# Sliding-window attention with a gated MLP on one core: query tiles of two 64-row blocks that lie 128 rows apart, 192 key columns each, in place of 128 consecutive queries with 256 columns

## The chip, the cores and the metric

The kernel runs on one core of a Trainium2 chip. The metric is the device time of one execution in microseconds; the number before is the median of three runs.

## The reference

```python
# q, k, v: batch 8, heads 8, sequence 576, head size 64
rel  = pos[:, None] - pos[None, :]
mask = (rel >= 0) & (rel < 128)
scores = where(mask, q @ k.T / 8 - slope[h] * abs(rel), -1e9)
x = (softmax(scores) @ v).transpose(0, 2, 1, 3).reshape(8, 576, 512)
h = relu(x @ w_in)                  # 512 -> 1024
u, v = h[..., :512], h[..., 512:]
v_n = (v - mean(v)) / sqrt(var(v) + 1e-6)
v_s = einsum('ts,bsd->btd', w_spatial, v_n) + b_spatial[None, :, None]
out = (u * v_s) @ w_out             # 512 -> 512
```

Each query sees itself and the 127 keys before it. A block of 64 queries therefore needs at most 192 keys, a block of 128 consecutive queries at most 256.

## The kernel before, in words

The work of a batch falls into four attention units (one for each pair `p` of heads; `j` is the head in the pair) and a gated part. 576 queries are cut into five tiles of 128, the last of 64. Scores are f32 products with the 64 head dimensions on the partitions, so that both heads and two halves of a query tile fit into the array side by side.

An attention unit of batches 1 to 7 goes through `scores`, `products` and `attention`:

- PE writes the scores of all five tiles in one piece of work (line 641), in blocks of 64 queries and up to 192 keys. Tiles 0 and 1 share one PSUM bank per head, tiles 2 and 3 another (buffers `s`, four of them), and tile 4 takes a buffer `x` (batches from 2 on; in batch 1 it takes `s`). The parts of a 256-column row that no product writes were set to zero once at the start (line 302).
- DVE reads a tile's scores, adds the table of slope and mask for the head (`tabs`), writes the sum to `prob` and keeps the row minimum (line 652). ACT takes the exponential in place, with the row sum (line 658). Both read 128, 256, 256, 256 and 192 columns.
- DVE adds a small constant and takes reciprocals (lines 681, 685). ACT writes the f16 rounding of the normalised probabilities to `pq` (line 693), DVE the remainder (line 698).
- SP transposes all of `pq` of a head by DMA into `pt` (line 704).
- PE multiplies with V in f16 parts (line 737): three products (high and low part of V, high and low part of the probabilities) for each of the seven ranges in `WINDOWS`, which lie in the transposed columns, and for both heads. ACT and DVE split the result into two f16 halves `xt` (lines 746, 750).

Batch 0 and the first pair of batch 1 (the pairs in `RAW` and `first`) take another way, `raw_tile` and `raw_rest`: one tile of one head pair at a time, scores in 128-query products (line 545), `prob` normalised in f32 (lines 577, 578), transposed on PE (line 587), copied to SBUF (line 316) and multiplied with V in f32 (line 605). Beside these tiles run the preparation of the weights, on DVE and ACT.

The gated part (`gated`) holds PE's large products: `v_unit` (line 802), `v_rem` (824), `u_unit` (854), `sp_unit` (875) and `o_unit` (901), with the layer norm (`layer_norm`) between them.

Nothing is issued in source order. Each piece of work is entered in a `Plan` with its engine, an estimated cost, a due time and what it reads and writes. `emit` lists the pieces forwards and backwards 20 times by a model of the engines, with these costs and PE's clock rule in it, and keeps the order that the model ends first. `either` gives a piece two engines, and the model picks one. Costs that a piece is entered with therefore steer the order on all engines and on SP's queue.

Of the kernel before, what the change touches and what calls it, by code (L numbers as in the profile page):

```python
# [9 lines left out]
F32 = mybir.dt.float32  # L10
# [19 lines left out]
MASKED = -2.0 ** 33  # L30
# [143 lines left out]
def attn_gmlp_kernel(ctx, tc, qk, v, w_in, w_spT, b_sp, w_out, outT):  # L174
# [5 lines left out]
    P = 2 * D  # L180
# [26 lines left out]

    RAW = {(0, p) for p in range(4)} | {(1, p) for p in range(1)}
# [8 lines left out]
    plan.kept["s"] = [ps.tile([P, 2, 2 * P], F32, name=f"s{k}") for k in range(4)]  # L217
# [23 lines left out]
    ones = fixed([P, P], BF16, "ones")  # L241
    powers = fixed([P, 2], F32, "powers")
    wpowers = fixed([P, 2], F32, "wpowers")
    tabs = [fixed([P, 2 * P], BF16, f"tab{h}") for h in range(H)]
# [9 lines left out]
    NB = 2 * NQ - 1  # L254
    OFF = [0] + [(2 * t - 1) * P for t in range(1, NQ)]
    prob = [fixed([P, NB * P], F32, f"prob{j}") for j in range(4)]
# [12 lines left out]
    relf = plan.buf(work, "u", 7, [P, 2 * P], F32)  # L269
    maskt = plan.buf(work, "u", 7, [P, 2 * P], F32)  # L270

    def constants():
        def f():
            nc.gpsimd.iota(relf(), [[-1, 2 * P]], base=P, channel_multiplier=1, allow_small_or_imprecise_dtypes=True)
        plan.add("POOL", 400, 0, f, (), [(relf, 0)])

        def f():
            nc.vector.memset(maskt(), 0.0)
        plan.add("DVE", dve(256), 0, f, (), [(maskt, 0)])

        def f():
            nc.gpsimd.affine_select(maskt(), maskt(), [[-1, 2 * P]], ALU.is_ge, MASKED, base=P, channel_multiplier=1)
            nc.gpsimd.affine_select(maskt(), maskt(), [[1, 2 * P]], ALU.is_ge, MASKED, base=-1, channel_multiplier=-1)
        plan.add("POOL", 800, 1, f, [(maskt, 0)], [(maskt, 0)])

        def f():
            nc.vector.memset(ident(), 1.0)
            nc.vector.memset(ones(), 1.0)
            nc.vector.memset(powers()[:, 0:1], 2.0 ** -13)
# [5 lines left out]
        plan.add("DVE", dve(400), 500, f, (), [(ident, 0), (ones, 0), (powers, 0), (wpowers, 0), (nhalf, 0)] + [(rstat, k) for k in range(8)])  # L295
# [5 lines left out]
        for k in range(4):  # L301
            plan.add("DVE", 340, 100, lambda k=k: nc.vector.memset(plan.kept["s"][k][:, 1, :], 0.0))
# [4 lines left out]
        for h in range(H):  # L307
            def f(h=h):
                slope = 2.0 ** (-8.0 * (h + 1) / H)
                nc.vector.scalar_tensor_tensor(tabs[h](), relf(), -8.0 * slope, maskt(), ALU.mult, ALU.add)  # L310
            plan.add("DVE", dve(256), 1000 + h * 4000, f, [(relf, 0), (maskt, 0)], [(tabs[h], 0)])
# [218 lines left out]

    def raw_tile(b, p, t, raw, vb, xt, slot, due, sums=None):

        m, k0, k1 = min(P, S - t * P), max(0, (t - 1) * P), min(S, (t + 1) * P)
        n, c0 = k1 - k0, P if t == 0 else 0
        blocks = [(k, min(P, k1 - k)) for k in range(k0, k1, P)]
        row, NM, SM, TM, RC = (slot + 4 * (t % 2)) % 8, 0, 2, 4, 6
        st = lambda k, j: rstat()[:m, row, k + j:k + j + 1]
        sc = [plan.buf(ps, "s", 4, [P, 2, 2 * P], F32) for _ in range(2)]
        pr = [lambda j=j: prob[2 * (t % 2) + j]()[:m, slot * 2 * P:slot * 2 * P + n] for j in range(2)]
        cols = [parts(prob[2 * (t % 2) + j], slot * 2 * P, slot * 2 * P + n) for j in range(2)]  # L540

        def f():
            for j in range(2):
                rows = slice(j * D, (j + 1) * D)
                nc.tensor.matmul(sc[j]()[:m, 0, :n], raw()[rows, 0, t * P:t * P + m], raw()[rows, 1, k0:k1], start=True, stop=True)
        plan.add("PE", SWITCH // 2 + pe(*[4 * n]), due, f, [(raw, k) for k in range(k0 // P, t + 1)], [(sc[j], 0) for j in range(2)])
        for j in range(2):
            h = 2 * p + j

            def f(j=j, h=h):  # L550
                nc.vector.tensor_tensor_reduce(pr[j](), sc[j]()[:m, 0, :n], tabs[h]()[:m, c0:c0 + n], -0.125, 3e38,
                                               ALU.add, ALU.min, st(NM, j))
            plan.add("DVE", dve(n), due + 300, f, [(sc[j], 0), (tabs[h], 0)], cols[j] + [(rstat, row)])
# [14 lines left out]
    def raw_rest(b, p, t, vb, xt, slot, due, row):  # L568
        m, k0, k1 = min(P, S - t * P), max(0, (t - 1) * P), min(S, (t + 1) * P)
        n = k1 - k0  # L570
        blocks = [(k, min(P, k1 - k)) for k in range(k0, k1, P)]
        RC = 6
        st = lambda k, j: rstat()[:m, row, k + j:k + j + 1]
        pr = [lambda j=j: prob[2 * (t % 2) + j]()[:m, slot * 2 * P:slot * 2 * P + n] for j in range(2)]
        cols = [parts(prob[2 * (t % 2) + j], slot * 2 * P, slot * 2 * P + n) for j in range(2)]
# [4 lines left out]
        tp = plan.buf(ps, *(("m", 2) if b == 0 else ("s", 4)), [P, 2, 2 * P], F32)  # L580
        flat = lambda: tp().rearrange("p a b -> p (a b)")

        def f():
            for i, (k, w) in enumerate(blocks):
                for j in range(2):
                    c = (2 * i + j) * m
                    nc.tensor.transpose(flat()[:w, c:c + m], pr[j]()[:, i * P:i * P + w], ident()[:m, :m])
# [426 lines left out]
```

## Time and profile before

| | |
|---|---|
| median of 3 runs | 585.93 us (585.79 to 586.01) |
| profiled execution | 588.65 us, span 586.9 us |
| PE busy | 554.9 us (95%), 5359 matmuls |
| DVE busy | 497.7 us (85%) |
| ACT busy | 436.9 us (74%) |
| POOL busy | 49.4 us (8%) |
| mean granted TensorE clock | 0.985 |

The span is the time from the first to the last instruction of the profiled execution. A busy share is a mean over stages with different limits, so the stages are looked at one by one below. A matmul's own duration holds its way through the array; neighbours overlap, and the price of one is read from the distance of starts.

### The profile page before, as it was taken

Reading aid. Unit: us, or ns where it says so; the run is one execution under the profiler, and the core shown is the slowest. Engines: PE = TensorE matmul, PEld = TensorE weight load, DVE = VectorE, ACT = ScalarE, POOL = GpSimd, SP = SyncE. Lnnn points to the kernel's source line nnn. Section 1 sums busy time; section 2 is a strip of 40 time slices with the busy share of each in tenths; the row PEclk is TensorE's granted clock in tenths of the full one; section 3 lists DMA queues with packets and bytes.
Section 4 is the critical chain, followed back from the end, with each engine's and each line's share of the span. In section 5 each row is a group of like instructions: output and inputs, shape, how many; then the busy total and the mean of one; then the engine's idle time right before and its main releaser. Section 6 shows DMA issues by size and latency. Waiting matters only on the chain.

```text
span 586.9 us, 14767 instructions
## 1 busy us (share of the span) xinstructions
PE 554.9 (95%) x5359; PEld 413.6 (70%) x5359; DVE 497.7 (85%) x1800; ACT 436.9 (74%) x1379; POOL 49.4 (8%) x108
## 2 busy tenths in 40 slices
PE   3699698999899999999999999999999999999997
PEld 2365346789477876888578957787688957886787
DVE  7989989998899989987998889888999789944650
ACT  5979979996887788877797769779797758743202
POOL 2110021002110001000110001100101011000100
PEclk9999689999899999999999999999999999999999
DMA  8944022489857862694768862886384744451002
GB/s 314 316 172 157 4 91 77 111 194 215 183 104 123 235 160 82 123 231 133 135 124 214 170 150 75 135 222 158 79 155 102 181 92 83 82 120 43 1 11 71
DMA packets 149997, 79.64 MB, mean 136 GB/s; under 512 B 129826, under 2 KB 140066, under 8 KB 149924
## 3 DMA queue, kind: packets, MB, share of 16 engines
q1 hardware_dynamic: 149924, 78.70, 55.4%
q8 instruction: 42, 0.69, 0.5%
q14 instruction: 31, 0.25, 0.2%
HBM read 37.13 MB, written 9.44 MB: 79 GB/s over the span
## 4 chain that ended last, share of the span: by engine, by line
PE 40%; DVE 7%; ACT 3%; DMA 2%; issue 1%; ACTq 0%; DVEq 0%
PE m L875 11%; PE m L901 10%; PE m L854 8%; PE m L802 4%; PE x L737 4%; PE s L641 3%; DMA pt<-pq 2%; DVE st L763 1%; DVE prob L652 1%; ACT junk L516 1%; DVE vt L776 1%; PE m L824 1%; DVE pq L698 1%; DVE vn L813 1%; DMA out_dram<-o 1%
## 5 line engine op out<-in xcount | busy, mean ns | idle before, releaser
L658 ACT ACTIVATE prob<-prob,stat 64x192 f32<-64x192 f32 (+2 forms) x270 | 124.9, 466 | 33.3 <-DVE stat L652 33.1
L875 PE MATMUL m<-wsp,vn 128*128 128x288 f16 x768 | 113.0, 286 | 0.6 <-DVE u L883 0.6
L901 PE MATMUL m<-gs,wout 128*128 128x288 f32 x768 | 110.8, 300 | 0.3 <-DVE o L909 0.3
L693 ACT ACTIVATE pq<-prob,stat 128x128 f16<-128x128 f32 (+1 forms) x270 | 105.8, 467 | 4.3 <-DVE stat L685 4.1
L698 DVE SCALAR_TENSOR_TENSOR pq<-prob,stat,pq 128x128 f16<-128x128 f32 (+1 forms) x270 | 103.5, 435 | 4.0 <-ACT pq L693 3.8
L901 PEld LDWEIGHTS m<-gs,wout 128*128 128x128 f32 x768 | 103.4, 189 | 3.3 <-issue 1.7
L854 PE MATMUL m<-xt,win 128*128 128x288 f16 x768 | 101.3, 286 | 0.9 <-ACT vt L320 0.4
L802 PE MATMUL m<-win,xt 128*128 128x512 f16 x384 | 92.0, 393 | 2.8 <-ACT o L908 2.0
L854 PEld LDWEIGHTS <-win 128*128 128x128 f16 x768 | 73.9, 98 | 24.1 <-issue 4.2
L875 PEld LDWEIGHTS <-vn 128*128 128x128 f16 x768 | 73.1, 98 | 21.7 <-issue 2.9
L652 DVE CUSTOM_DVE_ANT_0 prob<-s,tab 128x256 f32<-128x256 f32 (+2 forms) x222 | 73.1, 380 | 0.1
L802 PEld LDWEIGHTS <-xt 128*128 128x128 f16 x384 | 36.9, 100 | 48.4 <-issue 8.7
L772 POOL TENSOR_TENSOR st<-st,nhalf 128x1 f32<-128x1 f32 (+1 forms) x40 | 25.1, 627 | 315.6 <-DVE st L768 249.2
L658 ACT ACTIVATION_READ_ACCUMULATOR prob<-prob,stat 128x1 f32 (+1 forms) x270 | 51.3, 190 | 0.0
L883 DVE TENSOR_TENSOR u<-m,u 128x288 f32<-128x288 f32 x64 | 28.8, 450 | 23.8 <-PE m L875 23.8
L908 ACT ACTIVATE o<-m,am 128x288 f32<-128x288 f32 x42 | 20.9, 499 | 33.1 <-PE m L901 22.1
L737 PE MATMUL x<-pt,vh 128*64 128x256 f16 (+6 forms) x756 | 42.2, 229 | 1.1 <-DMA pt<-pq 1.0
L641 PE MATMUL s<-qkraw 64*64 64x192 f32 (+2 forms) x876 | 40.2, 310 | 0.0
L320 ACT ACTIVATE u<-m 128x288 f32<-128x288 f32 x57 | 22.9, 401 | 21.1 <-PE m L854 20.9
L737 PEld LDWEIGHTS <-vh 128*64 128x64 f16 x756 | 32.3, 110 | 8.3 <-issue 8.1
L763 DVE BATCH_NORM_STATS2 st<-vt 128x6 f32<-128x512 f32 (+1 forms) x40 | 27.5, 687 | 11.8 <-ACT vt L320 11.5
L737 PE MATMUL x<-pt,vl 128*64 128x256 f16 (+6 forms) x378 | 35.5, 228 | 0.0
(150 smaller groups left out, 808.6 us busy)
## 6 DMA issues: line engine op xcount, KB each, us to landing
qkraw<-in_qk_dram SPq DMA_DIRECT2D x28, 576.0 KB, 4.2
vb<-in_v_dram SPq DMA_DIRECT2D x32, 320.0 KB, 5.8
out_dram<-o SPq DMA_DIRECT2D x64, 144.0 KB, 2.0
vn<-in_w_in_dram SPq DMA_DIRECT2D x8, 512.0 KB, 6.8
pt<-in_w_out_dram SPq DMA_DIRECT2D x4, 512.0 KB, 6.5
gs<-in_w_spT_dram SPq DMA_DIRECT2D x4, 288.0 KB, 8.0
qkraw<-in_qk_dram SPq DMA_DIRECT2D x3, 320.0 KB, 5.4
pt<-pq SPq DMA_TRANSPOSE x54, 4.8
```

Source lines behind the costliest of these rows:

```text
L641: nc.tensor.matmul(sc[k][j]()[out, i, a - k0:z - k0], raw()[rows, 0, q:q + D], raw()[rows, 1, a:z], start=True, stop=True, skip_group_chec ...
L652: nc.vector.tensor_tensor_reduce(pt(), sc()[:m, i, :n], tabs[h]()[:m, c0:c0 + n], -0.125, 3e38, ALU.add, ALU.min, st()[:m, NM, j, t:t + 1])
L658: nc.scalar.activation(pt(), pt(), AF.Exp, bias=st()[:m, NM, j, t:t + 1], scale=-1.0, accum_out=st()[:m, SM, j, t:t + 1])
L693: nc.scalar.activation(pq[j]()[:m, 0, cs], prob[2 * (p % 2) + j]()[:m, cs], AF.Copy, scale=st()[:m, RC, j, t:t + 1])
L698: nc.vector.scalar_tensor_tensor(pq[j]()[:m, 1, cs], prob[2 * (p % 2) + j]()[:m, cs], st()[:m, RC, j, t:t + 1], pq[j]()[:m, 0, cs], ALU.mu ...
L737: nc.tensor.matmul(xp()[j * D:(j + 1) * D, x0:x0 + n], l()[:, kt, j * D:(j + 1) * D], rhs[:, o:o + n], start=j not in seen, stop=False, sk ...
L763: nc.vector.bn_stats(st()[:m, 0:6], vt()[:m])
L802: nc.tensor.matmul(pt(), xt[c]()[:, X0[a] + t * P:X0[a] + (t + 1) * P], win()[:, c, w, DH:DF], start=(n == 0), stop=(n == 3 * NC_ - 1))
L854: nc.tensor.matmul(pt()[:, :HS], win()[:, c, w, d * P:(d + 1) * P], xt[c]()[:, X0[a] + hf * HS:X0[a] + (hf + 1) * HS], start=(n == 0), sto ...
L875: nc.tensor.matmul(pt()[:, :HS], l, r, start=(n == 0), stop=(n == len(ops) - 1))
L883: nc.vector.tensor_tensor(u(), pt()[:, :HS], u(), ALU.mult)
L901: nc.tensor.matmul(pt()[:, :HS], wout()[:, d, w, e * P:(e + 1) * P], gs[d]()[:, a, :], start=(n == 0), stop=(n == 3 * ND - 1))
```

## The change: other query tiles

With nine blocks of 64 queries (0 to 8), the tiles become block 0 alone, and the pairs (1, 3), (2, 4), (5, 7) and (6, 8). The two blocks of a pair lie 128 rows apart, so that both have their keys in ranges of 192 columns that begin at different keys but have the same place relative to the queries; one table serves both. There are still five tiles. Block 1 has only 128 keys; the 64 columns ahead of them are filled by a small bf16 product (`ones` with `masked`), once per head.

```diff
+    TILES = ((0,), (1, 3), (2, 4), (5, 7), (6, 8))
+    W = P + D
+    POFF = (0, D, D + W, D + 2 * W, D + 3 * W)
+    QOFF = (0, 3 * D, 6 * D, 11 * D, 14 * D)
+    QGAPS = ((0, 3 * D), (9 * D, 11 * D), (17 * D, 18 * D))
+    SOFF = (0, D, D + W, 0, W)
...
-            nc.gpsimd.iota(relf(), [[-1, 2 * P]], base=P, channel_multiplier=1, allow_small_or_imprecise_dtypes=True)
...
-            nc.gpsimd.affine_select(maskt(), maskt(), [[-1, 2 * P]], ALU.is_ge, MASKED, base=P, channel_multiplier=1)
-            nc.gpsimd.affine_select(maskt(), maskt(), [[1, 2 * P]], ALU.is_ge, MASKED, base=-1, channel_multiplier=-1)
...
+            for a in (0, D):
+                rel = relf()[a:a + D]
+                nc.gpsimd.iota(rel, [[-1, W]], base=P, channel_multiplier=1, allow_small_or_imprecise_dtypes=True)
+                nc.gpsimd.affine_select(rel, rel, [[-1, W]], ALU.is_ge, FAR, base=P, channel_multiplier=1)
+                nc.gpsimd.affine_select(rel, rel, [[1, W]], ALU.is_ge, FAR, base=-1, channel_multiplier=-1)
...
-        for k in range(4):
-            plan.add("DVE", 340, 100, lambda k=k: nc.vector.memset(plan.kept["s"][k][:, 1, :], 0.0))
...
-                nc.vector.scalar_tensor_tensor(tabs[h](), relf(), -8.0 * slope, maskt(), ALU.mult, ALU.add)
-            plan.add("DVE", dve(256), 1000 + h * 4000, f, [(relf, 0), (maskt, 0)], [(tabs[h], 0)])
+                nc.gpsimd.tensor_scalar(tabs[h](), relf(), -8.0 * slope, None, ALU.mult)
...
+                nc.vector.tensor_scalar(tabs[h](), relf(), -8.0 * slope, None, ALU.mult)
+            plan.either([("DVE", dve(W, True), fv)] + [("POOL", pool(W), f)] * (h > 1), 1000 + h * 1000, [(relf, 0)], [(tabs[h], 0)])
...
+    def keys(i):
+        return max(0, i - 2) * D, (i + 1) * D
+
+    def scored(sc, t, off, raw):
+
+        for x, i in enumerate(TILES[t]):
+            k0, k1 = keys(i)
+            at = off + (W if t else D) - (k1 - k0)
+            out = slice(x * D, (x + 1) * D)
+            for j in range(2):
+                rows = slice(j * D, (j + 1) * D)
+                if at > off:
+                    nc.tensor.matmul(sc[j]()[out, off:at], ones()[rows, :D], masked()[rows], start=True, stop=True, skip_group_check=True)
+                nc.tensor.matmul(sc[j]()[out, at:at + k1 - k0], raw()[rows, 0, i * D:(i + 1) * D], raw()[rows, 1, k0:k1],
+                                 start=True, stop=True, skip_group_check=True)
+
+    def scored_ns(t):
+        return 107 if t == 0 else 360 if t == 1 else 320
...
+        plan.add("PE", SWITCH // 2 + scored_ns(t), due, lambda: scored(sc, t, 0, raw), seen_by(raw, t) + [(ones, 0), (masked, 0)], [(sc[j], t) for j in range(2)])
...
-        if len({w for _, w in blocks}) == 1:
-            e = len(blocks) * 2 * m
-            copy(e, lambda: (pf(P, 0, e), flat()[:, :e]), due + 1500, [(tp, 0)], pcols)
...
+        if t:
+            copy(2 * m, lambda: (pf(slice(0, P), 0, 2 * m), tp()[:, 0:2 * m]), due + 1500, [(tp, 0)], pcols[:len(pcols) // 2])
+        copy(2 * m, lambda: (pf(half, 2 * m, 4 * m), tp()[0:D, 2 * m:4 * m]), due + 1500, [(tp, 0)], halves)
...
-    BANKS = (((0, 1), ("s", 4)), ((2, 3), ("s", 4)), ((4,), ("x", 2)))
-
-    WINDOWS = (((0, 0, 256, 0), (1, 256, 160, 128), (2, 512, 32, 256)),
-               ((1, 416, 96, 0), (2, 544, 224, 0), (3, 768, 192, 96), (4, 1024, 64, 224)))
+    MOVES = ((0, 2, 0, 1, 2), (0, 0, 0, 0, 1), (0, 1, D, 3, 1), (1, 2, D, 3, 2), (1, 4, 0, 2, 1), (2, 4, D, 4, 1),
+             (1, 5, 0, 5, 1), (2, 6, 0, 5, 2), (2, 5, D, 7, 1), (3, 6, D, 7, 2), (3, 8, 0, 6, 1), (4, 8, D, 8, 1))
...
-                d = due - 4500 + (t if len(banks) < 3 or t < NQ - 1 else -1) * 700 + j * 200
...
+                d = due - 4500 + t * 700 + j * 200
...
-        for g, banks in enumerate((BANKS,) if b >= WHOLE else (BANKS[:2], ((BANKS[2][0], ("s", 4)),))):
+        for g, banks in enumerate((((0, 1, 2), (3, 4)),) if b >= WHOLE else (((0, 1, 2),), ((3, 4),))):
...
+            for kt, chunk, c, i, n in MOVES:
+                xp, x0 = xps[i > 4], (i - 5 * (i > 4)) * D
+                for l, a in ((vh, 0), (vh, 1), (vl, 0)):
+                    for j in range(2):
+                        rhs = pts[j]()[:, a * NB + chunk:a * NB + chunk + n, c:c + D]
+                        nc.tensor.matmul(xp()[j * D:(j + 1) * D, x0:x0 + n * D], l()[:, kt, j * D:(j + 1) * D], rhs,
+                                         start=(i > 4, j) not in seen, stop=False, skip_group_check=True)
+                        seen.add((i > 4, j))
...
-            qs = slice(hf * HS, (hf + 1) * HS)
+            q0, q1 = ((0, 5 * D), (5 * D, S))[hf]
```

A move is (key tile, first 128-column chunk of the transposed probabilities, column in the chunk, first query block, number of query blocks): 12 of them, four with two blocks and eight with one, take the place of the seven windows. `pq` keeps its size of nine times 128 columns per part, with gaps (`QGAPS`) that `clear` zeroes once on POOL in three pieces for each head in place of one; so the transposes keep theirs. All five tiles of a unit now have their scores in the `s` buffers, (0, 1, 2) in one pair of banks and (3, 4) in the other. The result of the V products is split at query 320 in place of 288. In `raw_rest` the transposed probabilities of a tile come as one full part of 128 keys and one half part of 64, copied separately, and the V products go block by block: four steps of 64 queries for each head, two with 128 keys and two with 64. Costs in the plan are those of the new shapes.

More of the change, by code (lines that the diff above doesn't have):

```diff
@@ L214, in attn_gmlp_kernel @@
     plan = Plan()
-    plan.kept["s"] = [ps.tile([P, 2, 2 * P], F32, name=f"s{k}") for k in range(4)]
+    plan.kept["s"] = [ps.tile([P, 4 * P], F32, name=f"s{k}") for k in range(4)]
     def fixed(shape, dtype, name):
@@ L542, in f @@
[L542 to L546, printed above, removed]
+        sc = [plan.buf(ps, "s", 4, [P, 4 * P], F32) for _ in range(2)]
+        pr = [lambda j=j: prob[2 * (t % 2) + j]()[:m, slot * W:slot * W + n] for j in range(2)]
@@ L547, in raw_tile @@
+        cols = [parts(prob[2 * (t % 2) + j], slot * W, slot * W + n, D) for j in range(2)]
+        plan.add("PE", SWITCH // 2 + scored_ns(t), due, lambda: scored(sc, t, 0, raw), seen_by(raw, t) + [(ones, 0), (masked, 0)], [(sc[j], t) for j in range(2)])
         for j in range(2):
@@ L579, in raw_rest @@
                         due + 1000, cols[j] + [(rstat, row)], cols[j])
-        tp = plan.buf(ps, *(("m", 2) if b == 0 else ("s", 4)), [P, 2, 2 * P], F32)
-        flat = lambda: tp().rearrange("p a b -> p (a b)")
+        tp = plan.buf(ps, *(("m", 2) if b == 0 else ("s", 4)), [P, 4 * P], F32)
+        half = slice(D, P) if odd else slice(0, D)
+        cf, ch = (D, 0) if odd else (0, P if t else 0)
         def f():
[L584 to L587, printed above, removed]
@@ L610, in raw_rest @@
-        copy(m, lambda: (xt()[:, qs], xp()[:, :m]), due + 2000, [(xp, 0)], xh)
+                    c = (a + j) * m + x * D
+                    nc.tensor.matmul(xp()[j * D:(j + 1) * D, x * D:(x + 1) * D], vb()[rows, p, k, j * D:(j + 1) * D], pf(rows, c, c + D),
+                                     start=j not in seen, stop=False, skip_group_check=True)
+                    seen.add(j)
+        plan.add("PE", SWITCH // 2 + (4 if t else 1) * 120, due + 1800, f, pcols + [(vb, p)], [(xp, 0)])
+        xh, xl = ([k for i in tile_ for k in xcols(xt, a, i * D, (i + 1) * D)] for a in range(2))
@@ L633, in products @@
-        span = [(k, i, t, min(P, S - t * P), max(0, (t - 1) * P), min(S, (t + 1) * P)) for k, (ts_, _) in enumerate(banks) for i, t in enumerate(ts_)]
+        sc = {t: pair for ts_ in banks for pair in [[plan.buf(ps, "s", 4, [P, 4 * P], F32) for _ in range(2)]] for t in ts_}
         def f():
-            for k, i, t, m, k0, k1 in span:
-                for q in range(t * P, t * P + m, D):
-                    for j in range(2):
-                        rows, out = slice(j * D, (j + 1) * D), slice(q - t * P, q - t * P + D)
-                        a, z = max(k0, q - P), q + D
-                        nc.tensor.matmul(sc[k][j]()[out, i, a - k0:z - k0], raw()[rows, 0, q:q + D], raw()[rows, 1, a:z],
-                                         start=True, stop=True, skip_group_check=True)
```

158 lines of the change are left out of this document (78 added, 80 removed).

## The prediction

> **What bounds the kernel now.** I read the page first, then busy time by stage, then the chain that ended last.
>
> ```profile
> span 586.9 us, 14767 instructions
> PE 554.9 (95%) x5359; PEld 413.6 (70%) x5359; DVE 497.7 (85%) x1800; ACT 436.9 (74%) x1379; POOL 49.4 (8%) x108
> ```
>
> ```profile
> core 0: us, PE busy (x) PEld busy (x) DVE busy (x) ACT busy (x) POOL busy (x), PEclk, DMA share, GB/s
> 0.00:60.00 60.00, 44.78 (x266) 26.23 (x266) 52.50 (x215) 49.81 (x159) 7.05 (x21) 1.00 0.66 235
> 60.00:100.00 40.00, 31.46 (x216) 18.76 (x216) 36.30 (x118) 36.44 (x101) 6.81 (x12) 0.83 0.20 63
> 100.00:165.00 65.00, 62.40 (x667) 46.10 (x666) 60.80 (x237) 57.18 (x194) 6.75 (x13) 0.97 0.69 159
> 165.00:520.00 355.00, 354.10 (x3713) 273.04 (x3713) 321.61 (x1168) 278.45 (x898) 26.00 (x57) 1.00 0.64 140
> ```
>
> There are two regimes. From 165 to 520 us PE is busy 354.10 of 355 us and DVE 321.61: only PE's own work counts there. Before 165 us PE is busy 138.6 and idle 26.4 us, while DVE is busy 149.6 and ACT 143.4: this stage is set by DVE and ACT, with PE waiting for them.
>
> ```profile
> 436.63 1.51 PE x L737 x42
> ...
> 439.71 1.72 PE m L875 x14
> ...
> 442.89 1.35 PE s L641 x28
> 444.25 0.21 PE x L641 x4
> 444.46 1.82 PE m L875 x14
> ...
> 449.61 1.59 PE m L901 x12
> 451.19 1.73 PE m L875 x14
> ```
>
> These rows are the chain in the PE stage (start, us, line, matmuls). Of an attention unit (a head pair of a batch) it holds 1.56 us of scores (L641) and 1.51 us of products with V (L737), 27 times. Everything else of the unit is DVE and ACT work beside PE.
>
> **Part 1, scores on PE.** Key columns of the live blocks are the same as before. They run as 64x64 tiles in four quarters of the array; L641 writes query blocks to an upper and a lower half. Before, the upper half gets blocks 0,2,4,6,8 = 64+4x192 = 832 columns, the lower 704. After, the pairs (1,3), (2,4), (5,7), (6,8) put 64+128+3x192 = 768 in one and 4x192 = 768 in the other. So 64 columns leave the longer half.
>
> ```profile
> 436.91 0.31 PE L737 MATMUL x<-pt,vh 128*64 128x160 f16 x4
> ...
> 437.12 0.21 PE L737 MATMUL x<-pt,vh 128*64 128x32 f16 x4
> ...
> 437.21 0.26 PE L737 MATMUL x<-pt,vh 128*64 128x96 f16 x4
> ...
> 437.34 0.36 PE L737 MATMUL x<-pt,vh 128*64 128x224 f16 x4
> ...
> 437.62 0.33 PE L737 MATMUL x<-pt,vh 128*64 128x192 f16 x4
> ...
> 437.87 0.23 PE L737 MATMUL x<-pt,vh 128*64 128x64 f16 x4
> 437.93 0.20 PE L737 MATMUL x<-pt,vl 128*64 128x64 f16 x2
> ```
>
> Each window here is three pairs of matmuls (both heads at once). 224 columns take (437.62-437.34)/3 = 0.093 us, so a column is about 0.42 ns. An f32 product counted as four such streams costs 1.7 ns a column: 832 x 1.7 = 1.41 us of the 1.56 measured, which fits. 64 columns less are -0.11 us. The new fill (one bf16 matmul of 64 columns per head, in block 1's empty key range) lies in the same half: 0.03 to 0.04 us by the 64-column rows. I take -0.07 us a unit, 27 x 0.07 = **-1.9 us**; ends -3.0 (fill hidden) and +0 (fill and its weight load 0.11).
>
> **Part 2, products with V on PE.** Before: 7 windows x 3 = 21 pairs, 1024 x 3 columns. After: 12 moves x 3 = 36 pairs, the same columns, as 12 pairs of 128 and 24 of 64. 32 columns take (437.21-437.12)/3 = 0.030 us, 64 columns take (437.93-437.87)/2 = 0.030. So there is a floor near 0.03 us a pair, and 64 columns nearly fill it. 128 columns lie between 96 (0.13/3 = 0.043) and 160 (0.21/3 = 0.070): 0.055. 12 x 0.055 + 24 x 0.031 = 1.40 us. The present windows take 0.21, 0.09, 0.13, 0.28, 0.25 and 0.09 by the rows, and the one of 256 columns 3 x (256 x 0.42 ns + 5 ns) = 0.34: together 1.39. The difference is 0.01 x 27 = **+0.3 us**. Ends: 0.028 a pair gives -1.6 us, 0.032 gives +1.0. The moving data are now 64-column pieces of 128-column chunks; no row has such a stride, and I take it at nothing because the four 128-column moves are two pieces of unbroken 64; if it cost the floor again per piece it would be 12 x 0.005, under 2 us in all.
>
> **Part 3, DVE and ACT.**
>
> ```profile
> L658 ACT ACTIVATE prob<-prob,stat 128x256 f32<-128x256 f32 x162 | 80.0, 497 | 0.3 <-DVE stat L652 0.3
> L658 ACT ACTIVATE prob<-prob,stat 64x192 f32<-64x192 f32 x54 | 24.2, 448 | 32.8 <-DVE stat L652 32.8
> L658 ACT ACTIVATE prob<-prob,stat 128x128 f32<-128x128 f32 x54 | 21.0, 391 | 0.1
> L693 ACT ACTIVATE pq<-prob,stat 128x256 f16<-128x256 f32 x162 | 71.6, 498 | 0.0
> L693 ACT ACTIVATE pq<-prob,stat 64x192 f16<-64x192 f32 x54 | 24.0, 445 | 0.0
> L693 ACT ACTIVATE pq<-prob,stat 128x128 f16<-128x128 f32 x54 | 21.3, 395 | 4.3 <-DVE stat L685 4.1
> L698 DVE SCALAR_TENSOR_TENSOR pq<-prob,stat,pq 128x256 f16<-128x256 f32 x162 | 70.2, 475 | 0.1
> L698 DVE SCALAR_TENSOR_TENSOR pq<-prob,stat,pq 64x192 f16<-64x192 f32 x54 | 22.0, 407 | 0.0
> L698 DVE SCALAR_TENSOR_TENSOR pq<-prob,stat,pq 128x128 f16<-128x128 f32 x54 | 18.4, 341 | 3.9 <-ACT pq L693 3.8
> L652 DVE CUSTOM_DVE_ANT_0 prob<-s,tab 128x256 f32<-128x256 f32 x162 | 60.1, 414 | 0.0
> L652 DVE CUSTOM_DVE_ANT_0 prob<-x,tab 64x192 f32<-64x192 f32 x48 | 15.2, 345 | 4.8 <-PE x L641 4.8
> L652 DVE CUSTOM_DVE_ANT_0 prob<-s,tab 128x128 f32<-128x128 f32 x54 | 13.3, 280 | 0.0
> ```
>
> Behind the bar stand the busy time in us and the mean of one in ns (80.0 and 497). Per head the five tiles were one of 128, three of 256 and one of 192 columns; they become one of 64 and four of 192, still five. The 64-column price is carried on from the step 256 to 128 (half of it off the 128 row). L658: 2330 to about 2132; L693: 2334 to 2125; L698: 2173 to 1902; L652: 1867 to 1593. So -0.41 us ACT and -0.55 us DVE a head: over 54 heads -22 and -29 us of busy time. In the PE stage that is worth nothing: PE covers it. Were that cover gone, DVE at 321.6 of 355 us would be next.
>
> It counts before 165 us. Batch 1's three units of this kind give 6 heads: DVE -3.3, ACT -2.4. The 25 raw tiles of batch 0 and of batch 1's first pair:
>
> ```profile
> L316 ACT COPY pq<-m 128x512 f32<-128x512 f32 x10 | 5.7, 584 | 0.3 <-PE m L587 0.3
> L316 ACT COPY pq<-m 128x256 f32<-128x256 f32 x2 | 0.7, 346 | 0.0
> L310 DVE SCALAR_TENSOR_TENSOR tab<-u 128x256 bf16<-128x256 f32 x8 | 3.2, 436 | 0.5 <-POOL u L283 0.5
> L302 DVE MEMSET s<- 128x256 f32 x4 | 1.1, 272 | 0.1
> ```
>
> Score reads on DVE, 30 x 0.069 + 10 x 0.067 = -2.7. Exponentials on ACT, 40 x 0.05 = -2.0; normalising the same, half on each. One copy of 512 columns becomes two of 256: 2 x 346 - 584 = +0.11, 15 times, and the last tiles' narrow copies become wide (about +0.8): +2.4, half on each. Tables: 192 columns and one operand fewer, 8 x 436 ns less a quarter at least (-0.9), all of it gone to POOL at most (-3.5); I take -1.5. Four bank memsets go, -1.1. In all DVE -5.1, ACT -1.8; with batch 1 -8.4 and -4.2, a mean of **6.3 us** a side. As neither engine alone sets the stage and PE's wait also holds loads, I pass half of it on: **-3.2 us**; ends 0 and -6.3. POOL's mask building becomes six short operations in place of three and the clearing of gaps three memsets in place of one; POOL is 8% busy, and nothing but the first table waits for it. SP issues the same loads and transposes of the same size, in whatever order the planner now puts them. Raw products with V now change from 128-row to 64-row form in each tile. A change of form costs 1.82-1.72 = 0.10 us (first L875 after L641 against one in a run): 25 x 0.10 = 2.5 us of PE, beside its 26.4 us idle.
>
> **Part 4, the last unit.**
>
> ```profile
> PE x L737 <- DMA pt<-pq: 1.0, 1, 1.0
> ```
>
> This is PE's only long wait after 165 us, for the last unit's transposed probabilities; two heads' DVE and ACT work ahead of it is a microsecond shorter. I take **-0.5 us**, ends 0 and -1.0. Should PE catch up, the layer-norm chain after it is late next.
>
> Sum: -1.9 + 0.3 - 3.2 - 0.5 = -5.3 us. The profiled execution has a span of 586.9 and a time of 588.65 us, so 581.6 and 583.3; the median shown is 585.93, 2.7 below that execution, and gives **580.6 us**.
>
> **The rivals.** *More than that.* The DVE and ACT saving passes on whole and the half-clock stretch goes too:
>
> ```profile
> 71.66 5.30 PE L802 MATMUL m<-win,xt 128*128 128x512 f16 x12 [0.78 <-DVE pq L316]
> ...
> 79.50 2.76 PE L802 MATMUL m<-win,xt 128*128 128x512 f16 x12
> ```
>
> The same twelve matmuls took 5.30 us after PE's long waits, 2.76 later (granted clock 0.83 in that stage). -6.3 - 2.5 - 2.1 = -10.9: 575.0 us. Against it: PE still has to wait for the first loads and weights.
>
> *Nothing.* Early waits stay where they are since each is one chain, V products cost their upper end, the fill takes back most of the scores' gain: within 0.2% (584.8 to 587.1), which is about what a measurement of this kernel can tell from no change. The 26.4 us of idle speak against it.
>
> *Slower: the fill drains PE.* It puts bf16 between f32 matmuls. If each border cost what a change of form costs, 0.10 us, the four borders of two heads give 0.40 x 27 = +10.8 us, and 591.4 us. It decides from 5.3/27 = 0.20 us a unit. Against: L901 in f32 and L875 in f16 alternate at 1.59 and 1.73 against 1.72 in a run, some 0.01 us a border. The Trainium skill (TensorEngine Tiling (Array Packing), Tiling Modes) says that changing the tiling mode, not just the tile, drains the engine; the fill keeps the 64x64 mode, and by that rule this rival's price would be nothing and the sum would stand. The 0.10 us row agrees with it where the form does change.
>
> *Slower: weight loads bind.* A load row of L737 lasts 0.110 us; with two in flight a pair could start every 0.055, 36 x 0.055 = 1.98 us, +0.58 x 27 = +15.7 and 596.3 us. Against: six loads of the 32-column window pass in 0.09 us. The Trainium skill (TensorE: Matmul & The Clock Gate, LDWEIGHTS) prices a load at its columns over 1.2 GHz; by an estimate from that, 64 columns take 53 ns and this rival would give nearly its time; the rows of 0.030 us a pair do not bear it out.
>
> **How the numbers follow.** Forecast (576.5 to 584.7) 0.66; more than that 0.13; nothing 0.09; fill drains 0.06; loads bind 0.03; a worse order from the planner, with an early stall of some microseconds, 0.03. Faster 0.79, same 0.09, slower 0.12. The range 575.5 to 586.5 leaves out the slower cases and the lower half of the first rival. The forecast's own range is 576.5 to 584.7.
>
> **What the next profile would show.** Right: scores near 1.49 us and V products near 1.40 to 1.52 in the chain; no 128x256 rows on L652 and its kin, rows of 128x192 at the 64x192 prices; PE idle before 165 us down to about 23. Wrong: scores above 1.6 us (fill), V products near 2 us (loads), PE idle still 26, or a changed clock between 60 and 100 us. A new wait on POOL's tables at the start would show as a later first L551.

## Result and profile after

The changed kernel takes 588.65 us (median of five runs, 587.84 to 591.01) against 585.93 us for the kernel before (585.44 to 586.59): a ratio of 1.0052, interval 1.0027 to 1.0078. It is slower by half a per cent, where 580.6 us was forecast. The profiled execution took 587.84 us, so it is the quickest of its five; that of the kernel before took 588.65 us, 2.7 us above its median. The spans of the two profiles (586.1 and 586.9 us) therefore stand the other way round than the medians. One later run of the changed kernel (593.94 us), more than 1.5% above its fastest, is left out of the medians, ranges and ratios below.

The page after, first lines:

```profile
span 586.1 us, 16954 instructions
PE 551.9 (94%) x6453; PEld 415.6 (71%) x6453; DVE 470.9 (80%) x1809; ACT 411.6 (70%) x1381; POOL 56.1 (10%) x115
```

DVE is busy 26.8 us less than before (497.7) and ACT 25.3 less (436.9). Busy time of each engine by stage, as before:

```profile
0.00:60.00 60.00, 38.73 (x402) 22.82 (x402) 50.13 (x226) 53.48 (x182) 8.96 (x25) 0.99 0.70 235
60.00:100.00 40.00, 38.42 (x372) 25.29 (x373) 37.42 (x119) 36.41 (x106) 8.21 (x14) 0.85 0.19 63
100.00:165.00 65.00, 62.97 (x845) 47.63 (x844) 60.99 (x265) 61.07 (x220) 7.63 (x15) 1.00 0.90 194
165.00:520.00 355.00, 351.02 (x4346) 271.77 (x4344) 297.12 (x1142) 246.04 (x849) 28.52 (x56) 0.99 0.63 134
```

Two things are new. DVE is busy 297 us from 165 to 520 us instead of 322, and ACT 246 instead of 278, as the narrower tiles should make it. But PE, which was busy 354.10 of these 355 us, now is busy 351.02: it is idle for 4.0 us in a stage in which it had been idle for 0.9. That needs a cause.

The shares of 10 us from 170 us on show it (columns as above; the third from the right is the granted clock of PE), and the waits of the changed kernel name it (us in total, times, longest):

```profile
170.00:180.00 10.00, 8.73 (x129) 6.84 (x128) 6.32 (x32) 5.85 (x23) 0.33 (x1) 1.00 0.35 61
180.00:190.00 10.00, 7.51 (x99) 5.69 (x99) 6.83 (x19) 4.65 (x14) 2.20 (x6) 0.66 0.40 76
```

```profile
PE m L882 <- ACT u L325: 3.8, 1, 3.8
...
ACT pq L721 <- DMA pt<-pq: 4.3, 1, 4.3
```

PE stands still for 3.8 us and then runs at a granted clock of 0.66 in the mean over 10 us. The chain that ended last runs through this place (start, us, what):

```profile
173.90 1.55 PE x L765 x72
175.44 0.03 PE m L882
175.47 4.62 DMA pt<-pq
...
181.11 1.04 ACT pq L721 x3
182.15 0.30 ACT u L325
182.45 0.04 issue
182.49 3.04 PE m L882 x12
185.53 2.70 PE x L765 x40
```

Read it from the top. The products of one attention unit with V (line 765) end at 175.4 us. In that moment a transposing DMA starts, which lands 4.62 us later; only then may ACT write the next normalised tile to `pq` (line 721), behind which stands an eviction of the gated part (line 325), for which PE waits (line 882). What does a transpose have to do with the V products of another unit? It needs a buffer `pt`. There are three; a unit fills two. SP's own records say how long it stood there (start, us, engine, line, operation):

```profile
165.47 13.33 SPq L732 DMA_TRANSPOSE pt<-pq  x2
```

The two transposes of a unit were issued from 165.47 us on. The first took SP 2.72 us; the second started at 175.47 us, when the V products of the unit before, which read the buffer that it needs, were over. The price of the lower clock stands in twelve matmuls of the same line and shape a moment earlier and later:

```profile
175.38 1.64 PE L882 MATMUL m<-xt,win 128*128 128x288 f16 x12
...
182.49 3.04 PE L882 MATMUL m<-xt,win 128*128 128x288 f16 x12 [3.76 <-ACT u L325]
```

The planner lists the scores of a unit before the V products of the unit before it (`AHEAD = 1`), and a buffer's owners are known to it in the order of listing. So it does not know that the transpose has to wait for products listed later. It is the same in the kernel before; what it costs depends on the order that the planner happens to choose. There, after 165 us, PE waits behind it only at the last unit (1.0 us, see below).

### The profile page after: what moved, and what is told of

Same layout as the page of the kernel before. It is cut to its first block, busy times and chain, and to the rows that moved or that the text cites. A ratio compares the mean times of both kernels' runs of the same rounds, so it can differ in the third digit from the quotient of the medians.

```text
span 586.1 us, 16954 instructions
## 1 busy us (share of the span) xinstructions
PE 551.9 (94%) x6453; PEld 415.6 (71%) x6453; DVE 470.9 (80%) x1809; ACT 411.6 (70%) x1381; POOL 56.1 (10%) x115
## 4 chain that ended last, share of the span: by engine, by line
PE 69%; ACT 12%; DMA 9%; DVE 7%; issue 1%; SPq 1%; POOL 0%; ACTq 0%; DVEq 0%
PE m L903 16%; PE m L882 14%; PE m L929 14%; PE m L830 10%; PE x L765 7%; PE s L549 6%; DMA out_dram<-o 3%; DMA pt<-pq 3%; ACT prob L586 2%; ACT prob L687 2%; PE m L852 1%; DMA gs<-in_w_spT_dram 1%; ACT pq L721 1%; DVE prob L681 1%; ACT pq L321 1%
## 5 line engine op out<-in xcount | busy, mean ns | idle before, releaser
L687 ACT ACTIVATE prob<-prob,stat 64x64 f32<-64x64 f32 (+1 forms) x270 | 113.3, 423 | 16.7 <-DVE stat L681 16.6
L721 ACT ACTIVATE pq<-prob,stat 64x64 f16<-64x64 f32 (+1 forms) x270 | 93.8, 422 | 10.0 <-DMA pt<-pq 5.9
L726 DVE SCALAR_TENSOR_TENSOR pq<-prob,stat,pq 64x64 f16<-64x64 f32 (+1 forms) x270 | 91.2, 379 | 1.8 <-ACT pq L721 1.2
L681 DVE CUSTOM_DVE_ANT_0 prob<-s,tab 64x64 f32<-64x64 f32 (+1 forms) x270 | 72.7, 316 | 2.4 <-PE s L549 2.4
L549 PE MATMUL s<-qkraw 64*64 64x192 f32 (+2 forms) x1116 | 60.7, 325 | 8.2 <-DMA qkraw<-in_qk_dram 8.2
L549 PEld LDWEIGHTS s<-qkraw 64*64 64x64 f32 x1116 | 41.8, 137 | 20.2 <-issue 13.1
L687 ACT ACTIVATION_READ_ACCUMULATOR prob<-prob,stat 64x1 f32 (+1 forms) x270 | 51.1, 189 | 0.0
L765 PEld LDWEIGHTS <-vh 128*64 128x64 f16 x1296 | 41.0, 114 | 9.9 <-issue 9.5
L765 PE MATMUL x<-pt,vh 128*64 128x64 f16 (+1 forms) x1296 | 44.4, 207 | 2.4 <-DMA pt<-pq 2.4
L765 PE MATMUL x<-pt,vl 128*64 128x64 f16 (+1 forms) x648 | 41.1, 206 | 0.0
```

Of the source, the lines that this page charges most:

```text
L549: nc.tensor.matmul(sc[j]()[out, at:at + k1 - k0], raw()[rows, 0, i * D:(i + 1) * D], raw()[rows, 1, k0:k1], start=True, stop=True, skip_gr ...
L681: nc.vector.tensor_tensor_reduce(pt(), sc[t][j]()[:m, SOFF[t]:SOFF[t] + n], tabs[h]()[:m, W - n:], -0.125, 3e38, ALU.add, ALU.min, st()[:m ...
L687: nc.scalar.activation(pt(), pt(), AF.Exp, bias=st()[:m, NM, j, t:t + 1], scale=-1.0, accum_out=st()[:m, SM, j, t:t + 1])
L721: nc.scalar.activation(pq[j]()[:m, 0, qs], prob[2 * (p % 2) + j]()[:m, cs], AF.Copy, scale=st()[:m, RC, j, t:t + 1])
L726: nc.vector.scalar_tensor_tensor(pq[j]()[:m, 1, qs], prob[2 * (p % 2) + j]()[:m, cs], st()[:m, RC, j, t:t + 1], pq[j]()[:m, 0, qs], ALU.mu ...
L765: nc.tensor.matmul(xp()[j * D:(j + 1) * D, x0:x0 + n * D], l()[:, kt, j * D:(j + 1) * D], rhs, start=(i > 4, j) not in seen, stop=False, s ...
```

## Experiments

All times are medians; ratios are against the kernel before, run on the same chip in the same session, with 95% intervals.

### The two kernels again

> The kernel before, unchanged, for a second profile. The profile shown took 588.65 us, 2.7 above the median of its runs, and the changed kernel's profile 587.84. If the median run differs from the profiled one in one place, it should show here: a span near 584 us, and the place should be in the first 165 us, where PE is idle 26.4 us and the granted clock was 0.83 between 60 and 100 us. If span and idle time are as before (587, 26), the spread is not tied to a place.

> The changed kernel, unchanged, as the measure for the two below, since its five runs spread from 587.8 to 591.0. Buffer theory: the same stall as in the first profile (PE idle about 4 us between 170 and 190 us and half the clock after it), time 588 to 590. Price theory (its PE work per unit is dearer): the stall is chance and may be gone, with the time still 588.

Before once more (one execution): the span is 586.2 us, with 26.6 us of PE idle ahead of 165 us, so the spread is not tied to one place. PE is busy 54.92 of the 55 us from 165 to 220 us, so there is no stall to remove there. The kernel before with a fourth `pt` buffer was not run. After once more: 588.47 us (585.01 to 592.57), ratio 1.0050 [1.0028, 1.0072]. Its profiled execution was the quickest of its runs, and shows the same stall with another sequel:

```profile
182.27 1.63 PE L882 MATMUL m<-xt,win 128*128 128x288 f16 x12 [3.70 <-ACT u L325]
...
180.00:190.00 10.00, 7.73 (x121) 6.53 (x121) 8.94 (x25) 4.50 (x14) 3.11 (x6) 1.00 0.75 117
```

PE stood 3.70 us and went on at full clock: 1.63 us for the twelve matmuls. In the profile with block 0 between others (below) a stall of 3.69 us is followed by 2.21 us for the twelve. So a stall of this length sometimes costs its own length (585.0 us) and sometimes more, which fits the wide scatter of this kernel (7.6 us, against 4 for the kernel before). The granted clocks say the same: 0.991 in its quickest run and 0.977 in its slowest, and 0.014 of 585 us is 8.2 us (not all of it need come from this place). The Trainium skill (TensorE: Matmul & The Clock Gate, Part 1: The HAM clock gate) gives an idle window of about 3.4 us that runs freely, after which the clock is halved; 3.70 us with full clock behind it and 3.76 with half agree with a window whose phase is not the kernel's.

### A fourth buffer

> The changed kernel with four buffers for the transposed probabilities in place of three; the order of the instructions on every engine is the same. Buffer theory: the transpose at 176 us goes out about 10 us earlier, ACT isn't held at pq, PE's wait of 3.8 us at 179 us and the half clock behind it go; time 582 to 584. Price theory: the changed kernel loses on PE in every unit, and a fourth buffer changes nothing: 588 to 590.

```diff
-lambda: pool.tile(shape, dtype, tag=tag, name=tag, bufs=bufs)
+lambda: pool.tile(shape, dtype, tag=tag, name=tag, bufs=bufs + (tag == "pt"))
```

The planner is not told of it, so the order of the instructions is the same on every engine. 581.78 us (581.09 to 584.48), ratio 0.9935 [0.9914, 0.9956]: 6.7 us less than the changed kernel in the same session. SP's two transposes at that place, and busy time by stage:

```profile
167.97 5.96 SPq L732 DMA_TRANSPOSE pt<-pq  x2
```

```profile
165.00:220.00 55.00, 55.00 (x683) 43.22 (x682) 44.62 (x169) 35.41 (x122) 5.73 (x11) 1.00 0.63 146
220.00:520.00 300.00, 299.88 (x3764) 233.14 (x3760) 255.90 (x982) 214.50 (x738) 23.85 (x47) 1.00 0.66 138
```

SP is held 5.96 us instead of 13.33, PE is busy 55.00 of 55 us and keeps its clock. In the first profile the stall took 3.8 us and the clock behind it about 2.6 (7.51 us of work at 0.66); the last unit's wait of 1.6 us for its transposed tiles is gone as well. That is 8.0 us, where the spans of the two profiles differ by 6.1 (586.1 and 580.0): the one with four buffers had a granted clock of 0.80 from 60 to 100 us against 0.85, which is 2.0 us of these 40. This is the run that settles why the change was slower: the wait for a buffer, taken away by itself, turns +0.5% into -0.65%.

### Or telling the planner

> The changed kernel with three buffers, but each unit's products with V are entered in the plan ahead of the next unit's scores (AHEAD 0 in place of 1). So the plan knows that the second transpose of a unit waits for the products with V of the unit before, and orders accordingly. Buffer theory: the order no longer asks for a transpose that its buffer can't take, the stall near 180 us is gone without a fourth buffer, 582 to 584. Rival: what helped in the run with four buffers was the buffer alone, and with three the units are too close whatever the order: 586 to 589.

```diff
-    AHEAD = 1
+    AHEAD = 0
```

Three buffers, but each unit's V products are listed before the next unit's scores, so the wait is in the planner's model: 583.04 us, ratio 0.9951 [0.9934, 0.9969]. No stall either:

```profile
165.00:220.00 55.00, 54.68 (x627) 42.55 (x625) 44.17 (x163) 35.97 (x123) 4.91 (x8) 1.00 0.64 145
```

### Scores: block 0 between others

> The changed kernel with the scores of a unit issued in another order of blocks: 3, 1, 0, 2, 4, 5, 7, 6, 8 in place of 0, 1, 3, 2, 4, 5, 7, 6, 8; everything else keeps its place. Theory of the lone block: the array's lower half stands idle for the first 0.12 us of a unit, while block 0 runs alone, so the lower half ends last; with block 3 first the unit's scores fall from 1.57 to about 1.48 us, 27 units give -2.4 us where PE is the bound. Rival: the fill between the f32 products sets the length; then 1.57 stays and the time too.

The chain rows of one unit's scores in the changed kernel, then with the products in the order 3, 1, 0, 2, 4, ... of the query blocks:

```profile
310.04 0.28 PE s L549 x5
310.32 0.01 PE s L548
310.32 1.28 PE s L549 x29
```

```profile
309.16 0.16 PE s L549
309.31 0.01 PE s L548
309.32 1.34 PE s L549 x31
```

1.57 us become 1.51. In the first order block 0 comes first and alone. In the records, the lower half of the array then starts its first product 0.12 us behind the upper one (0.013 us in the kernel before), and since the halves now have 768 columns each, the late one sets the end. The whole time hardly moves with three buffers, 588.27 us, ratio 1.003 [1.0011, 1.0049]; the stall is still there (3.7 us at the same place).

> Four buffers and the block order 3, 1, 0, 2, ... together; order on all engines else as in the changed kernel. In the run with the block order alone the batches followed each other in 63.8 us in place of 64.0, which the stall covered in part. Now PE is the bound from the end of the weights on: 24 units at -0.065 us are -1.6 us, 580.2. If the shorter scores only move PE's wait elsewhere: 581.8 as with four buffers alone.

> As the one before, and from batch 3 on the fill of block 1's empty key range is left where it stands: the banks keep their roles and nothing else writes there. Takes away 40 small matmuls. Fill costs its stream (64 columns, 0.03 us a unit): -0.5 us, about 579.7. Fill drains PE at each border (0.1 us): -2 to -8. Fill hidden: no change.

With four buffers and this order: 581.23 us, ratio 0.9904 [0.988, 0.9929]. The estimate of 27 x 0.06 = 1.6 us fits the difference of the ratios (0.0031, or 1.8 us), but the interval overlaps that of four buffers alone, and the sessions differ. Without the fill of block 1 in batches 3 to 7, where the bank still holds what was filled earlier: 580.64 us, ratio 0.9905 [0.9884, 0.9925]. The fill costs nothing that can be measured. These two are the quickest versions found; the runs do not tell them apart.

### Does the early gain come from DVE and ACT?

In the changed kernel, batch 1 reaches the end of its first gated product (the v part, `v_unit`) 6 us earlier than before (table below). To see whether the narrower tiles' time on DVE and ACT makes that, it was given back, on tiles that nobody reads, with four buffers and the order of the other instructions unchanged on every engine.

> Four buffers, and behind each read of scores and each remainder of the probabilities a memset of one column on DVE (0.059 us in the first profile) into a tile that nobody reads: DVE gets about the busy time back that the narrower tiles had saved it (0.55 us a head, 6.6 us before 165 us), in the same order. If DVE sets the stage before 165 us and half of its time passes on, as the prediction took: 581.8 + 3.3 = 585. If all of it: 588. If the stage is set by chains and not by DVE's time: 582.

```diff
+nc.vector.memset(idle()[:, 0:1], 0.0)   # behind each score read and each remainder, 590 in all
```

583.11 us, ratio 0.9939 [0.9919, 0.9959], as four buffers alone. But the test was too weak: a memset lasts 59 ns in the records and adds only 8 to 10 ns from one operation's start to the next one's (278 to 286 ns at line 681, 329 to 339 at line 726). Of the expected cost only 1.6 us was put back ahead of 165 us.

> The version with four pt buffers, and behind each DVE read of a score tile and each DVE remainder a memset of 128x40 f32 into a tile that nobody reads, 590 in all; the order of the instructions on every engine stays. The one-column memset of the run before added only some 15 ns from start to start. With 40 columns it should add about 55 ns, which is what the narrower tile saves in such an operation (256 columns 344 and 396 ns from start to start, 192 columns 278 and 329). 165 of them fall before 165 us, some 9 us of DVE. If the early gain comes from DVE's narrower tiles, 4 to 8 of the 581.8 us come back (585.5 to 590, ratio 1.000 to 1.006). If it comes from ACT, or from the planner's other order, the time stays at 581 to 583 (ratio 0.991 to 0.995). Busy time of DVE rises by 30 us or more in both.

> The version with four pt buffers, and on ACT a copy of 128x16 f32 into a tile that nobody reads: one a head behind the exponentials of a unit and one behind its normalised tiles, one a tile of the units at the start. An ACT operation of 64 columns takes 245 ns from start to start and one of 192 takes 346, so one of 16 is estimated at 207 ns, as much as the narrower tiles save in five operations (207 ns by the start-to-start times 399, 347, 292, 346, 245). About 43 of them, 9 us of ACT, fall before 165 us, 120 or so in all. If ACT's narrower tiles make the early gain, the time goes to 585 to 590 (ratio 1.000 to 1.006); if DVE's do or the order, it stays at 581 to 583.

> Both additions together, the order of the instructions still that of four pt buffers. If the narrower tiles of DVE and ACT make the early gain, each covering for the other, all of it goes: 586 to 592 (ratio 1.000 to 1.010), with the last product of the third batch's out-projection at 264 us instead of 260. If the planner's other order makes the gain, 581 to 584 (ratio below 0.997).

```diff
+nc.vector.memset(idle(), 0.0)                                    # 128x40
+nc.scalar.activation(spare(), ident()[:, :16], AF.Copy, scale=1.0)
```

```profile
L685 DVE MEMSET idle<- 128x40 f32 x270 | 24.8, 92 | 0.0
```

Forty columns last 92 ns and still add only 8 to 12 ns, so the DVE part is as weak as the one before; the ACT copies last 204 ns and add 106, 4.6 us ahead of 165. DVE: 583.05 us (0.9954 [0.9934, 0.9974]); ACT: 582.85 (0.9957 [0.9936, 0.9979]); both: 585.37 (0.9992 [0.997, 1.0014]). The 0.9935 of four buffers lies within the first interval and at the edge of the second, so neither shows a cost; both together cost 3.3 us. That is between the theories: more than "the order alone", with less time put back than was meant.

> Four pt buffers, order unchanged on every engine; one DVE operation of 128x128 on tiles that nobody reads behind each head's score reads and one behind its remainders (estimated from the start-to-start times at 262 ns, where the narrower tiles save 266 ns in five operations), two for each unit at the start, and on ACT one copy of 128x128 at the places where the run before had 128x16 (some 200 ns, where the narrower tiles save 207). This is the time of the wide tiles on both engines with the narrow tiles' products and order. If the early gain is the narrower tiles' time on DVE and ACT, all of the gain of four buffers goes and a little more, since the products are no cheaper than before: 585.5 to 589 (ratio 0.9995 to 1.006). If only some 3.5 us of it, as with the smaller additions, 584.5 to 585.5. If the planner's order makes the gain, 581.5 to 583.

> The DVE operations of 128x128 alone, ACT as with four buffers. If DVE and ACT share the early stage, about half of what both together cost: 583 to 585 (ratio 0.995 to 0.998). If DVE sets the stage by itself: 585.5 or more. If ACT does: 581.5 to 582.5.

```diff
+nc.vector.scalar_tensor_tensor(idle(), ident(), nhalf()[:, 0:1], ident(), ALU.mult, ALU.subtract)
+nc.scalar.activation(spare(), ident(), AF.Copy, scale=1.0)
```

These operations do take time from start to start, 264 ns on DVE and 200 on ACT, 8.4 us ahead of 165 us on either engine (32 and 42 of them). DVE alone: 593.94 us, ratio 1.0144 [1.0122, 1.0166]; both: 596.56 us, 1.0179 [1.0158, 1.0199]. Both together cost more than any theory said (589 at most); DVE alone falls under "585.5 or more", but its 12.2 us are more than the 8.4 put back ahead of 165 us. The start of the last matmul of three pieces of work, and the granted clock of PE from 60 to 100 us, in the profiled execution of each kernel (one execution each; the spatial product is `sp_unit`):

| us from the start of the span | v part of batch 1 | spatial product, batch 1 | spatial product, batch 6 | clock, 60 to 100 us |
|---|---|---|---|---|
| before | 163.7 | 200.7 | 519.7 | 0.83 |
| before, again | 163.3 | 200.8 | 518.6 | 0.79 |
| after | 157.7 | 199.8 | 518.3 | 0.85 |
| after, again | 157.6 | 196.9 | 515.3 | 0.87 |
| four buffers | 160.2 | 195.8 | 513.9 | 0.80 |
| four buffers, one-column memsets | 156.7 | 192.7 | 512.6 | 0.87 |
| four buffers, DVE time back | 163.4 | 200.2 | 527.3 | 0.79 |
| four buffers, DVE and ACT time back | 166.3 | 203.2 | 530.3 | 0.79 |
| before, other order (170, below) | 161.2 | 198.7 | 518.2 | 0.86 |
| after, other order (170) | 162.1 | 198.3 | 515.5 | 0.84 |
| four buffers, other order (170) | 164.6 | 200.7 | 518.0 | 0.83 |

The clock in the last column shifts the first: 0.80 and 0.87 of 40 us differ by 2.8 us, and the two rows with four buffers and little or nothing put back, at these clocks, differ by 3.5. Rows can therefore be compared at like clocks alone. Before (again) and four buffers, at 0.79 and 0.80, are 3.1 us apart, not 6. With 8.4 us back on DVE, at 0.79, batch 1 is 3.2 to 4.4 us later than with four buffers at 0.80, with 8.4 on either side 6.1 to 7.4 (here the clock was also 0.97 ahead of 60 us, up to 1.8 us of it). So in this order the early stage does hang on DVE and ACT; how much of what a side gets it passes on, single executions do not fix. The last three rows forbid to go further: with the planner's price at 170 ns the kernel before is as early as the versions with narrower tiles, or earlier. Whether the gain by 165 us belongs to the tiles or to the order, these rows do not separate. The surprise is the other half of the loss, after 200 us. Busy time from 220 to 520 us with DVE's time back, and of the kernel before:

```profile
220.00:520.00 300.00, 294.53 (x3634) 223.21 (x3633) 270.07 (x1052) 212.84 (x736) 26.74 (x48) 1.00 0.62 134
```

```profile
220.00:520.00 300.00, 299.10 (x3136) 229.17 (x3130) 271.22 (x993) 235.88 (x763) 22.18 (x48) 1.00 0.62 136
```

DVE is as busy in the one as in the other (270 and 271 us), yet PE loses 5.5 us in the first and 0.9 in the second. The order of the first was chosen for tiles that take less DVE time, that of the kernel before for tiles that take more. PE's waits in the first are many and none is over 1.0 us; most are for DVE and ACT work of the gated part. Equal busy shares thus do not mean equal cover. That the order makes the difference is argued, not shown: the added operations also stand at other places than the time of the wider tiles.

### The order by itself

> Four pt buffers, the product sequence with block 0 inside, and the V products planned before the next unit's scores, so that the plan knows what each buffer waits for. If the three gains add: 578 to 580.5 (ratio 0.987 to 0.991). If the told dependency is worth nothing once there are four buffers: 581 (0.9905, as the other two alone). If its order is worse at the end, where the last unit has no other work beside it: 583.

583.81 us, ratio 0.9971 [0.9953, 0.9989]: the three gains do not add. Told of the dependency, the planner writes another order, and with four buffers that order is the slower one.

> The kernel before with one price in the planner's model lower, 170 in place of 190 ns for the change from one set of products to the next on PE. The instructions stay, and the planner, which searches by these prices, writes another order of them; by its own account the end moves from 570.9 to 569.9 us. If the order alone is worth little: within 1 us of before (ratio 0.998 to 1.002). If luck of the order is worth as much as what was seen here: 3 us or more to either side.

> Four pt buffers with the same lower price, so with another order again (570.9 for before, 559.3 for four buffers and 558.6 for this by the planner's account). If the gain of four buffers belongs to the tiles and not to one order: 579 to 584 (ratio 0.989 to 0.996). If it hung on one lucky order: 585 or more.

> The changed kernel, three pt buffers, with the planner's price for the change of products lowered as in the two orders before (its own account: 558.6 us). If the wait for a pt buffer that its model doesn't know belongs to this kernel's orders in general, there is again a stall of PE of some microseconds behind a transpose, and the time is 585 to 592 (ratio 0.999 to 1.010), above the 585.1 that the same price gave with four buffers. If the stall was of the one order only: 580 to 584 (ratio below 0.997).

> The kernel before with that price at 210 ns (the planner's account: 572.4 us). With 190 it takes 585.9 and with 170 it took 588.9. If orders of one kernel differ by some 3 us, 584 to 590 (ratio 0.997 to 1.007). A time near 581, as that of the narrower tiles with four buffers, would say that the tiles are worth nothing beside the order.

```diff
-    SWITCH = 190
+    SWITCH = 170        # 210 in the last one
```

| price of a change of products | before | after, three buffers | four buffers |
|---|---|---|---|
| 190 ns | 585.9 | 588.7 (1.0052 [1.0027, 1.0078]) | 581.8 (0.9935 [0.9914, 0.9956]) |
| 170 ns | 588.9 (1.0048 [1.003, 1.0065]) | 586.4 (1.003 [1.0006, 1.0054]) | 585.1 (0.9978 [0.9958, 0.9997]) |
| 210 ns | 586.5 (1.002 [1.0002, 1.0038]) | | |

The ratios are to the kernel before at 190. One number in the planner, and no instruction, moves a kernel by 0.6 to 3.3 us, to either side. The larger of these are as much as the change did. The planner's own account did not foresee it: it had the order with 170 a microsecond ahead of that with 190 for the kernel before, and it came out 3 us behind. The stall behind the third buffer belongs to one order: at 170 the changed kernel has none,

```profile
165.00:220.00 55.00, 55.00 (x593) 43.05 (x593) 43.15 (x158) 34.37 (x113) 6.86 (x13) 1.00 0.60 132
```

and yet takes 586.4 us, where 580 to 584 was expected of that case. Its profile shows smaller waits in other places, 35.88 us of PE in the 40 us before 100 and 37.83 in the 40 before 560, against 38.88 and 39.59 with four buffers at 190. Four buffers are ahead of the kernel before at both prices, by 4.2 and 3.8 us, but two orders of each are few, and how much of that is the tiles stays open to within the 3 us by which orders differ. The kernel before, with three buffers, also keeps its last unit's wait of 1.0 us, which a fourth might have taken away without any change of tiles.

## Why the prediction was wrong, point by point

**The step that failed** is one sentence of Part 3: that SP issues the same loads and transposes "in whatever order the planner now puts them", at no cost. In the order that came, the second transpose of a unit starts 10.0 us after the first, since no buffer is free, and PE loses 3.8 us and some more at a lower clock. Four buffers with the same order give 6.7 us back. The rival "a worse order from the planner, with an early stall of some microseconds" was there, at 0.03 and without a place. What pointed at the resource existed before: 54 transposes, three buffers, two to a unit, SP's waits, and the last unit's wait that Part 4 quotes. The chance was too small for a second reason: two other orders of the kernel before came out 0.2% and 0.5% slower, against the 0.9% that was forecast, so 0.79 for "faster" left too little to the order.

**Scores**: forecast 1.49 us, measured 1.57 (1.56 before). The count of columns was right (1.51 when block 0 stands between others), the order in the piece was not looked at: a lone block at the front leaves half of the array behind. +0.3 us in 27 units instead of -1.9. The fill, a suspect in the forecast, costs nothing measurable, so the first slower rival falls.

**Products with V**: forecast 1.52 us from 1.51, measured 1.55:

```profile
303.48 1.55 PE x L765 x72
```

```profile
303.41 0.30 PE L765 MATMUL x<-pt,vh 128*64 128x128 f16 x4
...
303.60 0.23 PE L765 MATMUL x<-pt,vh 128*64 128x64 f16 x4
...
303.69 0.23 PE L765 MATMUL x<-pt,vh 128*64 128x64 f16 x4
...
303.79 0.28 PE L765 MATMUL x<-pt,vh 128*64 128x128 f16 x4
...
303.96 0.23 PE L765 MATMUL x<-pt,vh 128*64 128x64 f16 x4
```

A pair of 64 columns takes (303.69-303.60)/3 = 0.030 to (303.79-303.69)/3 = 0.033 us, one of 128 takes (303.96-303.79)/3 = 0.057 to (303.60-303.41)/3 = 0.063, a little above the 0.055 taken. +1.1 us in all, the upper end. Two loads of 64 columns pass in those 0.030 us, so the rival of the loads falls. By an estimate from the Trainium skill (TensorE: Matmul & The Clock Gate, LDWEIGHTS), which prices a load at its columns over 1.2 GHz, one of 64 columns would take 53 ns; as the pace of these pairs the rows do not bear that out.

**DVE and ACT** prices were right: 448, 407 and 345 ns were taken for 128x192.

```profile
L687 ACT ACTIVATE prob<-prob,stat 128x192 f32<-128x192 f32 x216 | 95.1, 443 | 2.0 <-DVE stat L681 1.9
...
L726 DVE SCALAR_TENSOR_TENSOR pq<-prob,stat,pq 128x192 f16<-128x192 f32 x216 | 79.4, 407 | 0.4
...
L681 DVE CUSTOM_DVE_ANT_0 prob<-s,tab 128x192 f32<-128x192 f32 x216 | 64.9, 343 | 0.0
```

The busy time fell by 26.8 and 25.3 us (29 and 22 forecast). That half of the early 6.3 us passes on (3.2) is neither shown nor refuted as a size: at like clocks batch 1's v part came 3.1 us earlier with four buffers, which would fit, and giving the time back cost 3.2 for DVE and 6.1 for both; but another order of the kernel before is 2.5 us earlier without any of it. PE's idle time ahead of 165 us went from 26.4 to 24.9 us, less than the 23 named; busy time counts work at half clock and at full clock alike, so it was a poor sign.

**The last unit**: forecast -0.5 us; the wait for its transposed tiles grew from 1.0 to 1.6 us (1.3 and 1.7 in the second profiles).

```profile
PE x L765 <- DMA pt<-pq: 1.6, 1, 1.6
```

Part 4 put this wait down to the DVE and ACT work of two heads. The chains of before and after (start, us, what) show another cause: the transpose starts when the V products of the unit before end, as a wait for a buffer would have it.

```profile
519.98 1.51 PE x L737 x42
521.51 4.55 DMA pt<-pq
```

```profile
518.54 1.55 PE x L765 x72
520.12 5.12 DMA pt<-pq
```

With four buffers the profile of the changed kernel has no such wait.

With the sizes measured, +0.3 + 1.1 + 0.6 and an early gain of 3 to 6 us (3 at like clocks, 6 between the first two profiles) make -1 to -4 us without the stall, where -5.3 was forecast. With four buffers the last unit's 1.0 us goes too, which makes -2.6 to -5.6; in the same order they came to -4.2 (581.78 against 585.99). The parts were thus summed somewhat too high, and the one order that was run took all of it and 2.7 us more.

## What to carry to other kernels

Where a planner writes the order, every change of sizes is also a change of order: measure two or three orders of the kernel before and after (one price changed a little) before believing a difference under a per cent. Look for resources that the planner does not know, a buffer count above all, and either give one buffer more or list the work so that the wait is in the model; here that was worth more than the change itself. Do not read cover from busy shares: the same 270 us of DVE went with 0.9 us of idle PE in one order and with 5.5 in another. And before two profiles of an early stage are compared, compare their granted clocks there.

## What the runs showed of the hardware

- An operation's duration in the records is not what it takes from its engine. On DVE, 192 columns last 407 ns and start 329 ns apart (line 726), and a memset of 59 or 92 ns between two of them adds 8 to 12 ns; on ACT 443 and 346 ns, and a copy of 128x16 lasts 204 ns and adds 106.
- PE's clock after a stall of 3.7 to 3.8 us was lower in one profiled execution and full in another of the same kernel; the twelve matmuls after it took 3.04 and 1.63 us.
- The granted clock from 60 to 100 us was 0.80 and 0.87 in two executions with the same order on PE (four buffers, without and with one-column memsets), and the v part of batch 1 ended 3.5 us apart.
- In 64x64 tiles a half of the array that starts 0.12 us late stays behind, although both halves have as many columns: the piece took 1.57 us, and 1.51 with block 0 between others.
